# A linear-attention and SiLU kernel: first-layer blocks issued as two halves of 256 columns, finer zero matmuls, and a re-ordered start

## The chip, the cores and the metric

The kernel runs on one core of a Trainium2 chip. A core has a matrix engine (PE, whose weight loads are shown apart as PEld), a vector engine (DVE), a scalar engine (ACT), GpSimd (POOL) and a sync engine (SP), which here issues most of the transfers. Each engine takes its instructions in a fixed order; they meet only through semaphores. The metric is device time in microseconds (us) of one execution.

## The reference, cut to what matters

A decayed linear attention over 4 batches, 8 heads, 768 steps and 48 channels gives rows of 384 numbers. They go through a two-layer network with SiLU:

```python
y[:, :, t] = einsum('bhd,bhde->bhe', rt, state + u * kt (x) vt)
state      = w * state + kt (x) vt          # for t = 0 .. 767
x = y.transpose(0, 2, 1, 3).reshape(3072, 384)
h = x @ w_in                                # 384 -> 2048
out = (h * sigmoid(h)) @ w_out              # 2048 -> 384
```

`(x)` is the outer product over two channel axes. The output is 3072 x 384 in float32.

## The kernel before, in words

The 768 steps are cut into 6 chunks of 128. A *unit* is one chunk of one batch: unit i is chunk i // 4, batch i % 4, so there are 24. Each unit's r, k and v are loaded (`ld`, L71) into one of 8 buffers of each kind, r and k are turned by TensorE (`turn`, L352, transposes at L272), multiplied by powers of the decay on DVE (L289), multiplied with each other on TensorE (L380 for the first units, L455 later), masked, multiplied with v (L396, L552, L561), and added to a bonus term (`vu`) when they leave PSUM (L401). The bonus and the decayed k come from POOL (L240, L245, L248, L258), with a sum over channels on DVE in between (`bonus_sum`, L253).

The attention rows of a chunk are turned into x, 128 channels by 512 steps. For the first four units this is done on TensorE (`yT`, L591) and a copy out of PSUM (`copy_x`, L593); later by a transposing transfer (L584). The first layer then runs per block `ft` of 128 of the 2048 columns: three matmuls over the 384 channels into one PSUM bank (`l1_mm`, L601, L606), and one SiLU on ACT (L615). A block covers all four batches of the chunk, 512 columns (`first`, L679, for chunks 2 to 5), or two blocks at a time with two batches each, 256 columns per matmul (`halved`, L686, and `rest_first`, L676, for chunk 1; part of chunk 0). The second layer (L628) adds 16 matmuls of 384 columns per batch.

For the first six units the order of every instruction is written out by hand in the string `order` (L717). `T`, `P`, `V`, `yT` are TensorE steps, `rT`, `kT`, `n`, `e`, `rd` DVE steps, `ku`, `ru`, `kc`, `vu` POOL steps, `lr`, `lk`, `lv` loads of r, k, v on SP's queue, `v16` the cast of v to float16 on ACT, `pa` and `pd` the zeroing of a buffer's unused columns on ACT or on DVE, `tab` the load of the SiLU table on ACT, `L` and `G` a first-layer block's matmuls and its SiLU, `H` one entry of `halved`. `spin` (L178) issues matmuls of zeros, whose result is not used; the words `6*spin`, `1*spin`, `2*spin` place 15 of them, each of 512 columns.

From unit 6 on a loop takes two units at a time. It interleaves the attention's steps with first- and second-layer pieces from a queue, `fillers`, from which `fill(n)` (L668) pops n pieces in order: before the output matmuls (L782), after the loads (L801) and at two later places. SP's queue holds the loads in the order in which the program issues them, and each of them waits until the transfer issued eight places earlier has landed.

Of the kernel before, what the change touches and what calls it, by code (L numbers as in the profile page):

```python
# [8 lines left out]
FP = mybir.dt.float32  # L9
# [7 lines left out]
def kernel(  # L17
# [11 lines left out]
    nc = tc.nc  # L29

    B, H, S, D = r.shape
    C = 128
# [6 lines left out]
    NFT = DFF // 128  # L39
    NQ = HD // 128  # L40
# [7 lines left out]
    ps = ctx.enter_context(tc.tile_pool(name="ps", bufs=1, space=bass.MemoryType.PSUM))  # L48
    ctx.enter_context(tc.manual_schedule())

    def unit(i):
        return divmod(i, B)
# [15 lines left out]
    win = [big.tile([128, NQ, 512], F16, name=f"win{g}") for g in range(4)]  # L68
# [36 lines left out]
    idle = cst.tile([128, 512], F16)  # L105
# [53 lines left out]
    lamC = cst.tile([128, H, D], FP)  # L159
    lamH = cst.tile([128, H, D], FP)  # L160
# [4 lines left out]
    lamN = cst.tile([128, H, D], FP)  # L165
# [9 lines left out]
            nc.scalar.copy(out=dst[i][:, :, D:64],  # L175
                           in_=idle[:, 0:128].rearrange("p (h d) -> p h d", h=H))

    def spin(n):  # L178
        zs = ps.tile([128, 512], FP, name="zs", tag="moe", bufs=4)
        for _ in range(n):  # L180
            nc.tensor.matmul(zs, idle[:, 0:128], idle, start=True, stop=True)

    def clear():
        for t in att:
# [18 lines left out]
    def spread_row(name, src):  # L203
        spread[name] = ps.tile([128, HD], FP, name="bc", tag="moe", bufs=4)
        nc.tensor.matmul(spread[name], ones, src, start=True, stop=True)
# [91 lines left out]
    def by_planes(i):  # L297
        return i > 2 * B + 1
# [11 lines left out]
    def cast_k(i, copy=nc.scalar.copy):  # L310
        copy(out=kc[i % NIN][:, :, 0:D], in_=kd[i % 2].rearrange("p (h d) -> p h d", h=H))
# [155 lines left out]
    def sums(i):  # L467
        sc, b = unit(i)
        xs = range(2 if sc < NCH - 1 else 1)
        L(i)["sp"] = [ps.tile([128, 512], FP, name="sp", tag="moe", bufs=4) for _ in xs]  # L470
        for p in range(NP):
            for e in range(2):
                for x in xs:
                    rows = slice(HC * x, HC * x + HC)
                    for j in range(2):
                        h = 2 * p + j
                        c0 = (e * NP + p) * D
                        nc.tensor.matmul(L(i)["sp"][x][64 * j:64 * j + 64, c0:c0 + D],  # L478
                                         kc[(i + e) % NIN][rows, h, :],
                                         L(i + e)["v16"][rows, h, :],  # L480
                                         start=True, stop=True)
# [93 lines left out]
    xts = {}  # L575
# [23 lines left out]
    hpss = {}  # L599

    def l1_mm(sc, b0, nb, ft):  # L601
        m = B // nb
        hps = hpss[b0, ft] = ps.tile([128, m, nb * C], FP, name="hps", tag="moe", bufs=4)
        for f in range(m):
            for q in range(NQ):
                nc.tensor.matmul(hps[:, f, :].rearrange("p (b t) -> p b t", b=nb), win[(ft + f) // 4].rearrange("p q (t c) -> p q t c", c=4)  # L606
                                 [:, q, :, (ft + f) % 4],
                                 xts[sc][:, b0:b0 + nb, q, :],
                                 start=(q == 0), stop=(q == NQ - 1))

    def l1_silu(sc, b0, nb, ft):
        if sc not in gts:
            gts[sc] = wrk.tile([128, NFT, B * C], F16, name="gT", bufs=2)
        m = B // nb
        nc.scalar.activation(out=gts[sc][:, ft:ft + m, b0 * C:(b0 + nb) * C], in_=hpss[b0, ft],  # L615
                             func=AF.Silu)

    def l1(sc, b0, nb, ft):
        l1_mm(sc, b0, nb, ft)
        l1_silu(sc, b0, nb, ft)  # L620
# [47 lines left out]
    def fill(n):  # L668
        for _ in range(n):
            if fillers:  # L670
                fillers.pop(0)()
# [5 lines left out]
        return [lambda ft=ft: l1(sc, 2, 2, ft) for ft in range(0, NFT, 2)]  # L677

    def first(sc):  # L679
        return [lambda f=f: l1(sc, 0, B, f) for f in range(NFT)]  # L680

# [2 lines left out]
    halved = [lambda ft=ft: l1(1, 0, 2, ft) for ft in range(0, NFT, 2)]  # L686

    def piece(word, f):
        b0, ft = word.split(".")
        f(0, *blocks[b0], int(ft))  # L690
# [6 lines left out]
        "wy": lambda: columns(nc.scalar, wpT, w, 0), "lnw": powers_r, "eK": exponents_k,  # L697
        "lamK": powers_k, "uc": copy_u, "wb": lambda: spread_row("w", w_row),
        "ub": lambda: spread_row("u", u_row), "lnwb": ln_w, "lamC": powers_c, "lamH": powers_h, "lamN": powers_n,
        "tab": silu_table, "clear": clear, "spin": lambda: None, "H": lambda: halved.pop(0)(),  # L700
    }
    unit_steps = {
        "T": turn, "rT": lambda i: decay_one(i, 0), "kT": lambda i: decay_one(i, 1),
# [12 lines left out]
    }  # L716
    order = """  # L717
        ur kz0 id itr lr0 wy pd0 ak0 cz2 kz3 itc wr mk wx cz1 mh lnw eK cg3 lamK kz4 kz1 lk1
        id16 lr1 pd3 lr3 lk3 clear 6*spin lv0 cg0 lv1 kz7 lr2 ak2 ku0 lv3 lr5 kz2 lv2 ub pd1 lv4
        lr4 lk4 lv5 pd2 lk5 lk7 lr6 lk6 uc T0 1*spin T1 lr7 lv7 kT0 pa4 rT0 ru0 ku1  # L720
        v160 pd5 lv6 rT1 kz6 rd0 kT1 wb ru1 P0 n0 2*spin rd1 P1 vu0 lnwb T2 n1 v161 2*spin
        pd7 lamC lamH lamN pa6 i_q0 V0 v162 tab rT2 e0 kT2 ku2 T3 1*spin yT0 V1 kz5 vu1 i_q1 ru2
        xTD0 e1 P2 yT1 kT3 rd2 rT3 ku3 xTD1 P3 ru3 n2 rd3 v163 n3 L0.0 vu2 kc0 1*spin G0.0
        vu3 V2 L0.2 V3 G0.2 L0.4 e2 i_q2 e3 kc1 yT2 yT3 S0 G0.4 xT2 xTD3 kc2 L0.6 L2.4 G0.6
        st0 L2.0 scA0 v164 kc3 L2.6 ku4 i_q3 v165 L2.2 T4 rT4 kT4 G2.4 ru4 G2.2 T5 G2.0 G2.6
        L4.8 G4.8 L4.10 kT5 G4.10 L4.9 kc4 ku5 S2 L4.11 rd4 rT5 st2 sc2 kc5 sd4 ru5 G4.9
        G4.11 rA4 vu4 i_o0 Q4 D4 rA5 s1_4 ku7 L4.12 rd5 vu5 m4 s2_4 G4.12 L4.13 G4.13 T6 Z4
        L4.14 G4.14 L4.15 z4 yT4 2*spin yT5 i_o2 i_o1 ku6 xT4 xT5 rT6 T7 G4.15 rT7 v167 sd6
        kT6 v166 ru6 lr8 kc6 kc7 H H rd6 i_o3 H vu6 lr9 rP7 rA6 sn4 H H lk8 lk9 sx4 lv9 lv8
        ru7 kT7  # L730
    """
    for word in order.split():
        if "*" in word:
            n, word = word.split("*")
            spin(int(n))
        if word in steps:
            steps[word]()
        elif word[0] == "L":
            piece(word[1:], l1_mm)
        elif word[0] == "G":  # L740
            piece(word[1:], l1_silu)
        else:
            unit_steps[word[:-1]](int(word[-1]))
# [4 lines left out]
    for i in range(B + 2, NU, 2):  # L748
        sc, b = unit(i)
        nxt = range(i + 2, min(i + 4, NU))  # L750
        after = range(i + 4, min(i + 6, NU))
        split = i + 2 < NU and by_planes(i + 2)
        sums(i)
        product_halves(i)
        state_first(i)
        masked_halves(i)
        state_second(i)
        if by_planes(i + 4) and not by_planes(i):
            rescale_state(i)
        if i == B + 2:  # L760
            bonus_sum(i + 1)
            bonus_v(i + 1)
        if i == 2 * B:
            for n in nxt:
                split_k(n, nc.scalar.copy)
        if split:
            turn_planes()
        if b and split:
            for n in nxt:
                cast_k(n)  # L770
                cast_v(n)
        for n in nxt:
            bonus_products(n)
            if not split:
                decayed_k(n)
        if i > B + 2 or sc < NCH - 1:
            next_state(i)
        if not b and split:
            for n in nxt:
                cast_k(n, nc.gpsimd.tensor_copy)  # L780
                cast_v(n, nc.gpsimd.tensor_copy)
        fill(3 if b and split else 4)  # L782
        outputs_halves(i)
        next_crossed(i)
        for n in nxt:
            turn(n)
        evict_halves(i)
        turn_y_dma(i)
        if b:
            fillers.extend((first(sc) if sc > 1 else rest_first(sc)) + second(sc))  # L790
        for n in nxt:
            if split:
                decay_one(n, 0)
                if b:
                    join_k(n)
            else:
                decay(n)
        for dst, src in ((kin, k), (rin, r), (vin, v)):
            for n in after:
                ld(n, dst, src)  # L800
        fill(4)  # L801
        if i > 2 * B and not b and split:
            for n in nxt:
                join_k(n)
        for n in nxt:
            bonus_sum(n)
            if not split:
                cast_v(n)
            bonus_v(n)
        for n in after:  # L810
            weighted_k(n)
        if after and by_planes(i + 4) and not i == B + 2:
            for n in after:
                split_k(n)
        for n in nxt:
            fill(2)
            decay_r16(n, True)
        if i == 2 * B and split:
            for n in nxt:
                join_k(n)  # L820
        fill((5 if b and split else 4) if i < NU - 4 else 2)
# [31 lines left out]
```

## Time and profile before

| | us |
|---|---|
| median of 3 runs | 185.99 (183.11, 185.99, 186.72) |
| the profiled execution: its own time | 185.49 |
| its span, first to last instruction | 183.8 |
| PE busy in the span | 174.5 |
| POOL busy | 129.3 |
| DVE busy | 117.0 |
| ACT busy | 115.8 |

The profiled execution's own time is 1.69 us more than its span, which lies around it. Matmuls are pipelined: the duration of one holds the time until its result is out, so the cost of one in a row of many is the time from start to start. In the chain of waits each line has the start, the time that the piece adds to the chain, and what it is. In the timeline each line has start, length, engine, line and operation, and in brackets the time that the engine sat idle before it, with what ended the wait. A queue (SPq, POOLq) stands for the issuing of transfers.

### The profile page before, as it was taken

Reading aid. Unit: us, or ns where it says so; the run is one execution under the profiler, and the core shown is the slowest. Engines: PE = TensorE matmul, PEld = TensorE weight load, DVE = VectorE, ACT = ScalarE, POOL = GpSimd, SP = SyncE. Lnnn points to the kernel's source line nnn. Section 1 sums busy time; section 2 is a strip of 40 time slices with the busy share of each in tenths; the row PEclk is TensorE's granted clock in tenths of the full one; section 3 lists DMA queues with packets and bytes.
Section 4 is the critical chain, followed back from the end, with each engine's and each line's share of the span. In section 5 each row is a group of like instructions: output and inputs, shape, how many; then the busy total and the mean of one; then the engine's idle time right before and its main releaser. Section 6 shows DMA issues by size and latency. Waiting matters only on the chain.

```text
span 183.8 us, 6611 instructions
## 1 busy us (share of the span) xinstructions
PE 174.5 (95%) x2801; PEld 113.9 (62%) x2801; DVE 117.0 (64%) x231; ACT 115.8 (63%) x208; POOL 129.3 (70%) x179
## 2 busy tenths in 40 slices
PE   7977899999899999999899999999999999999993
PEld 2555786588666976656556555657656566555562
DVE  5999728897977985865775955776944974000120
ACT  4471787699145797398597488797588781299200
POOL 7999999898899979869979769879769700000000
PEclk9999999999999999999999999999999999999999
DMA  5999999899697799999599999499799201410022
GB/s 95 238 192 216 178 175 200 154 224 225 129 189 210 114 202 184 199 183 202 114 178 177 162 209 213 92 183 160 183 197 250 49 4 46 128 43 0 10 79 86
DMA packets 102865, 27.89 MB, mean 152 GB/s; under 512 B 97586, under 2 KB 102324, under 8 KB 102836
## 3 DMA queue, kind: packets, MB, share of 16 engines
q1 hardware_dynamic: 98224, 23.86, 66.5%
q0 software_dynamic: 2176, 3.15, 10.1%
q10 hardware_dynamic: 2436, 0.46, 1.3%
q8 instruction: 22, 0.36, 0.8%
q14 instruction: 7, 0.06, 0.1%
HBM read 20.45 MB, written 4.72 MB: 137 GB/s over the span
## 4 chain that ended last, share of the span: by engine, by line
PE 72%; POOL 17%; DMA 5%; issue 5%; ACT 0%; POOLq 0%
PE ops L628 33%; PE hps L606 26%; DMA kin<-in_k_dram 5%; PE att L455 4%; POOL ku L240 4%; POOL rku_f L245 3%; PE att L272 3%; POOL vu L258 2%; POOL kc L248 2%; PE yp L552 2%; PE sp L478 2%; PE ops L653 1%; PE yp L561 1%; POOL win L84 1%; POOL wout L89 1%
## 5 line engine op out<-in xcount | busy, mean ns | idle before, releaser
L606 PE MATMUL hps<-xT,win 128*128 128x512 f16 (+1 forms) x360 | 66.3, 338 | 0.1
L615 ACT ACTIVATE gT<-hps 128x512 f16<-128x512 f32 x96 | 55.3, 597 | 12.2 <-PE hps L606 8.9
L628 PE MATMUL ops<-wout,gT 128*128 128x384 f16 x368 | 62.9, 326 | 0.1
L606 PEld LDWEIGHTS <-win 128*128 128x128 f16 x360 | 39.0, 114 | 21.1 <-issue 0.4
L628 PEld LDWEIGHTS <-gT 128*128 128x128 f16 x368 | 35.0, 98 | 23.9 <-ACT gT L615 0.8
L401 DVE TENSOR_TENSOR y<-yp,vu 64x384 f16<-64x384 f32 (+1 forms) x34 | 18.9, 555 | 11.3 <-PE yp L561 5.5
L245 POOL TENSOR_TENSOR rku_f<-ku,u_bc 128x384 f32<-128x384 f32 x24 | 24.2, 1010 | 1.4
L240 POOL TENSOR_TENSOR ku<-kin,rin 128x384 f32<-128x384 f32 x24 | 24.2, 1007 | 0.7 <-DMA rin<-in_r_dram 0.6
L258 POOL TENSOR_TENSOR vu<-vin,rku 128x384 f32<-128x384 f32 x24 | 19.6, 828 | 6.8 <-DVE rku L253 6.8
L289 DVE TENSOR_TENSOR rT<-att,lamR 112x512 f16<-112x512 f32 (+1 forms) x26 | 17.8, 684 | 4.2 <-PE att L272 3.8
L326 ACT COPY kT<-blocks 112x1024 uint16<-112x1024 uint16 x14 | 15.6, 1160 | 7.6 <-DMA blocks<-planes 7.5
L634 ACT COPY osb<-ops 128x384 f32<-128x384 f32 x20 | 9.4, 475 | 16.5 <-PE ops L628 12.5
L495 DVE TENSOR_TENSOR s<-sp,sdec 112x384 f32<-112x384 f32 x10 | 5.6, 557 | 16.0 <-PE sp L478 15.4
L636 DVE COPY osb<-ops 128x384 f32<-128x384 f32 x3 | 1.7, 557 | 21.3 <-PE ops L628 21.3
L462 DVE TENSOR_TENSOR am<-att,maskH 128x1024 f16<-128x1024 f32 x10 | 12.2, 1224 | 3.5 <-PE att L455 3.5
L343 DVE TENSOR_TENSOR rX<-att,lamR 48x256 f16<-48x256 f32 x32 | 13.5, 421 | 0.5
L263 ACT CAST v<-vin 128x384 f16<-128x384 f32 x16 | 7.9, 510 | 8.4 <-DMA vin<-in_v_dram 8.3
L253 DVE TENSOR_REDUCE rku<-rku_f 128x8 f32<-128x384 f32 x24 | 12.4, 542 | 0.9 <-POOL rku_f L245 0.9
L314 POOL TENSOR_TENSOR lnw_bc<-kin,lamN 128x384 f32<-128x384 f32 x7 | 7.0, 1001 | 8.0 <-DMA kin<-in_k_dram 6.4
L434 ACT CAST s1h<-s 48x384 f16<-48x384 f32 x16 | 8.2, 510 | 6.7 <-DVE s L495 6.6
L455 PE MATMUL att<-rT,kT 48*64 48x64 f32 x640 | 11.9, 220 | 0.2 <-issue 0.2
L455 PEld LDWEIGHTS att<-rT,kT 48*64 48x64 f32 x640 | 10.6, 135 | 0.3 <-issue 0.3
(106 smaller groups left out, 214.0 us busy)
## 6 DMA issues: line engine op xcount, KB each, us to landing
rin<-in_r_dram SPq DMA_DIRECT2D x24, 192.0 KB, 4.0
vin<-in_v_dram SPq DMA_DIRECT2D x24, 192.0 KB, 4.6
out_dram<-osb SPq DMA_DIRECT2D x23, 192.0 KB, 3.2
kin<-in_k_dram SPq DMA_DIRECT2D x22, 192.0 KB, 3.5
win<-in_moe_w_in_dram POOLq DMA_DIRECT2D x4, 384.0 KB, 6.3
wout<-in_moe_w_out_dram POOLq DMA_DIRECT2D x4, 384.0 KB, 6.6
kin<-in_k_dram ACTq DMA_DIRECT2D x2, 192.0 KB, 3.7
xT<-y SPq DMA_TRANSPOSE x9, 2.8
```

Source lines behind the costliest of these rows:

```text
L240: eng.tensor_tensor(out=L(i)["ku"], in0=kin[i % NIN][:, :, 0:D], in1=rin[i % NIN][:, :, 0:D], op=ALU.mult)
L245: eng.tensor_tensor(out=L(i)["rku_f"], in0=L(i)["ku"], in1=u_bc, op=ALU.mult)
L253: nc.vector.tensor_reduce(out=L(i)["rku"], in_=L(i)["rku_f"], axis=mybir.AxisListType.X, op=ALU.add)
L258: eng.tensor_tensor(out=L(i)["vu"], in0=vin[i % NIN], in1=L(i)["rku"].unsqueeze(2).broadcast_to([128, H, D]), op=ALU.mult)
L289: nc.vector.tensor_tensor(out=L(i)[key].rearrange("p g (y t) -> p y g t", y=2), in0=L(i)["t"][0:PR, :, x], in1=lam, op=ALU.mult)
L326: nc.scalar.copy(out=L(i)["kT"].rearrange("p g t -> p (g t)").bitcast(U16) .rearrange("p (n y) -> p n y", y=2), in_=turned[0:PR, i % 2].re ...
L343: nc.vector.tensor_tensor(out=rx[here], in0=L(i)["t"][there, x, 0], in1=(lamM if by_planes(i) else lamR)[there, :, 0:HC], op=ALU.mult)
L401: nc.vector.tensor_tensor(out=y16[a], in0=y[b, 0:HD], in1=vu[a], op=ALU.add)
L455: nc.tensor.matmul(a[o0:o0 + HC, j, e, p, :], kT[r0:r0 + D, p, HC * x:HC * x + HC], rT[r0:r0 + D, p, HC * x:HC * x + HC], start=True, stop ...
L606: nc.tensor.matmul(hps[:, f, :].rearrange("p (b t) -> p b t", b=nb), win[(ft + f) // 4].rearrange("p q (t c) -> p q t c", c=4) [:, q, :, ( ...
L615: nc.scalar.activation(out=gts[sc][:, ft:ft + m, b0 * C:(b0 + nb) * C], in_=hpss[b0, ft], func=AF.Silu)
L628: nc.tensor.matmul(opss[b], gts[sc][:, ft, b * C:(b + 1) * C], wout[:, ft, :], start=(ft == 0), stop=(ft == NFT - 1))
```

## The change

1. A new function `l1_halves` replaces `l1` for the blocks of chunks 2 to 5 (16 blocks each): a block's three matmuls of 512 columns become six of 256, first for batches 0 and 1, then for batches 2 and 3, into the two halves of the same PSUM bank. The SiLU stays one instruction per block.
2. `spin` issues zero matmuls of 100 columns, five for each one before; the first six keep 512 columns (`long`). So nine of 512 become 45 of 100.
3. The start's order: `lv2` goes ahead of `lr5`; the zeroing of unit 7's columns goes from DVE to ACT (`pd7` to `pa7`); `v162` moves from before the table load to behind the two x copies; the x copies of units 0 and 1 go from DVE to ACT (`xTD` to `xT`); `rT3` goes ahead of `rd2`.
4. In the loop at unit 6, `fill` pops five pieces before the output matmuls instead of four, and three after the loads instead of four.

```diff
-    def spin(n):
+    def spin(n, cols=100):
         zs = ps.tile([128, 512], FP, name="zs", tag="moe", bufs=4)
-        for _ in range(n):
-            nc.tensor.matmul(zs, idle[:, 0:128], idle, start=True, stop=True)
+        for _ in range(n * (512 // cols)):
+            nc.tensor.matmul(zs[:, 0:cols], idle[:, 0:128], idle[:, 0:cols], start=True, stop=True)
...
+    def l1_halves(sc, ft):
+        hps = hpss[0, ft] = ps.tile([128, 1, B * C], FP, name="hps", tag="moe", bufs=4)
+        for b0 in range(0, B, 2):
+            for q in range(NQ):
+                nc.tensor.matmul(hps[:, 0, b0 * C:(b0 + 2) * C].rearrange("p (b t) -> p b t", b=2),
+                                 win[ft // 4].rearrange("p q (t c) -> p q t c", c=4)[:, q, :, ft % 4],
+                                 xts[sc][:, b0:b0 + 2, q, :],
+                                 start=(q == 0), stop=(q == NQ - 1))
+        l1_silu(sc, 0, B, ft)
...
     def first(sc):
-        return [lambda f=f: l1(sc, 0, B, f) for f in range(NFT)]
+        return [lambda f=f: l1_halves(sc, f) for f in range(NFT)]
...
-        id16 lr1 pd3 lr3 lk3 clear 6*spin lv0 cg0 lv1 kz7 lr2 ak2 ku0 lv3 lr5 kz2 lv2 ub pd1 lv4
+        id16 lr1 pd3 lr3 lk3 clear 6*long lv0 cg0 lv1 kz7 lr2 ak2 ku0 lv3 lv2 kz2 lr5 ub pd1 lv4
...
-        pd7 lamC lamH lamN pa6 i_q0 V0 v162 tab rT2 e0 kT2 ku2 T3 1*spin yT0 V1 kz5 vu1 i_q1 ru2
-        xTD0 e1 P2 yT1 kT3 rd2 rT3 ku3 xTD1 P3 ru3 n2 rd3 v163 n3 L0.0 ...
+        lamC lamH lamN pa6 pa7 i_q0 V0 tab rT2 e0 kT2 ku2 T3 1*spin yT0 V1 kz5 vu1 i_q1 ru2
+        xT0 e1 P2 yT1 kT3 rT3 rd2 ku3 xT1 v162 P3 ru3 n2 rd3 v163 n3 L0.0 ...
...
-            spin(int(n))
+            spin(int(n), *((512,) if word == "long" else ()))
...
-        fill(3 if b and split else 4)
+        fill(5 if i == B + 2 else 3 if b and split else 4)
...
-        fill(4)
+        fill(3 if i == B + 2 else 4)
```

More of the change, by code (lines that the diff above doesn't have):

```diff
@@ L699 @@
         "ub": lambda: spread_row("u", u_row), "lnwb": ln_w, "lamC": powers_c, "lamH": powers_h, "lamN": powers_n,
-        "tab": silu_table, "clear": clear, "spin": lambda: None, "H": lambda: halved.pop(0)(),
+        "tab": silu_table, "clear": clear, "spin": lambda: None, "long": lambda: None, "H": lambda: halved.pop(0)(),
     }
@@ L718 @@
         ur kz0 id itr lr0 wy pd0 ak0 cz2 kz3 itc wr mk wx cz1 mh lnw eK cg3 lamK kz4 kz1 lk1
-        id16 lr1 pd3 lr3 lk3 clear 6*spin lv0 cg0 lv1 kz7 lr2 ak2 ku0 lv3 lr5 kz2 lv2 ub pd1 lv4
-        lr4 lk4 lv5 pd2 lk5 lk7 lr6 lk6 uc T0 1*spin T1 lr7 lv7 kT0 pa4 rT0 ru0 ku1
-        v160 pd5 lv6 rT1 kz6 rd0 kT1 wb ru1 P0 n0 2*spin rd1 P1 vu0 lnwb T2 n1 v161 2*spin
-        pd7 lamC lamH lamN pa6 i_q0 V0 v162 tab rT2 e0 kT2 ku2 T3 1*spin yT0 V1 kz5 vu1 i_q1 ru2
[L723 to L730, printed above, removed]
+        id16 lr1 pd3 lr3 lk3 clear 6*long lv0 cg0 lv1 kz7 lr2 ak2 ku0 lv3 lv2 kz2 lr5 ub pd1 lv4
+        lr4 lk4 lv5 pd2 lk5 lk7 lr6 lk6 uc T0 1*spin T1 lr7 lv7 kT0 pa4 rT0 ru0 ku1 v160 pd5 lv6
+        rT1 kz6 rd0 kT1 wb ru1 P0 n0 2*spin rd1 P1 vu0 lnwb T2 n1 v161 2*spin lamC lamH lamN pa6
+        pa7 i_q0 V0 tab rT2 e0 kT2 ku2 T3 1*spin yT0 V1 kz5 vu1 i_q1 ru2 xT0 e1 P2 yT1 kT3 rT3
+        rd2 ku3 xT1 v162 P3 ru3 n2 rd3 v163 n3 L0.0 vu2 kc0 1*spin G0.0 vu3 V2 L0.2 V3 G0.2 L0.4
+        e2 i_q2 e3 kc1 yT2 yT3 S0 G0.4 xT2 xTD3 kc2 L0.6 L2.4 G0.6 st0 L2.0 scA0 v164 kc3 L2.6
+        ku4 i_q3 v165 L2.2 T4 rT4 kT4 G2.4 ru4 G2.2 T5 G2.0 G2.6 L4.8 G4.8 L4.10 kT5 G4.10 L4.9
+        kc4 ku5 S2 L4.11 rd4 rT5 st2 sc2 kc5 sd4 ru5 G4.9 G4.11 rA4 vu4 i_o0 Q4 D4 rA5 s1_4 ku7
+        L4.12 rd5 vu5 m4 s2_4 G4.12 L4.13 G4.13 T6 Z4 L4.14 G4.14 L4.15 z4 yT4 2*spin yT5 i_o2
+        i_o1 ku6 xT4 xT5 rT6 T7 G4.15 rT7 v167 sd6 kT6 v166 ru6 lr8 kc6 kc7 H H rd6 i_o3 H vu6
+        lr9 rP7 rA6 sn4 H H lk8 lk9 sx4 lv9 lv8 ru7 kT7
     """
```

## The prediction

> **What bounds the kernel now.** I read the page first, then the chain of waits, then the busy time in five stretches, and last the timelines of the start.
>
> ```profile
> span 183.8 us, 6611 instructions
> ...
> PE 174.5 (95%) x2801; PEld 113.9 (62%) x2801; DVE 117.0 (64%) x231; ACT 115.8 (63%) x208; POOL 129.3 (70%) x179
> ...
> PEclk9999999999999999999999999999999999999999
> ```
>
> PE is busy for 95% of the span at a granted clock of 9 tenths or more in every slice, so the idle 9.3 us are all that a better order could win. The stretches (length, busy time of each engine, granted clock, DMA) say where they lie:
>
> ```profile
> 0.00:5.60 5.60, 4.31 (x12) 1.62 (x12) 3.33 (x15) 2.94 (x7) 4.51 (x24) 1.00 0.67 124
> 5.60:22.30 16.70, 13.82 (x268) 10.21 (x267) 15.42 (x29) 8.26 (x19) 16.55 (x23) 1.00 1.12 208
> 22.30:48.20 25.90, 24.73 (x522) 19.35 (x522) 18.76 (x37) 19.68 (x39) 23.91 (x29) 1.00 1.05 192
> 48.20:180.80 132.60, 131.60 (x2004) 82.75 (x2004) 79.53 (x152) 84.68 (x144) 84.32 (x106) 1.00 0.71 140
> ```
>
> From 48.2 to 180.8 PE works 131.6 of 132.6 us: there each ns added to a matmul is added to the end. From 5.6 to 22.3 it idles 2.9 us, and POOL works 16.55 of 16.70: that stretch is POOL's. From 22.3 to 48.2 PE idles 1.2 us. The last 3.0 us are a copy and a store, which the change does not touch. The chain of waits has the pieces that price the change:
>
> ```profile
> 38.46 9.68 DMA kin<-in_k_dram
> 48.14 0.04 issue
> 48.19 0.44 PE att L272 x8
> 48.62 7.91 PE ops L628 x48
> ...
> 59.94 0.66 PE hps L606 x6
> ...
> 61.83 4.71 PE hps L606 x42
> ...
> 101.51 0.43 issue
> ...
> 159.99 10.36 PE hps L606 x48
> ```
>
> The reader is to see that the chain runs through POOL and one load of k until 48.14 and through PE alone behind it, and that L606 stands in it with both sizes: x42 and x6 are matmuls of 256 columns (chunk 1), x48 is of 512.
>
> **Part by part.**
>
> *Halves.* Chunks 2 to 5 have 4 x 16 blocks of 3 matmuls, 192 of 512 columns; they become 384 of 256. From the chain, 512 columns cost 10.36 / 48 = 215.8 ns from start to start, and 256 columns 4.71 / 42 = 112.1 ns. The form is the same as that of the new function: two batches, a new weight for each matmul, half a PSUM bank. A pair costs 224.2 ns, 8.4 more, and 192 x 8.4 ns = +1.61 us, nearly all behind 48.2 where PE has no slack. Bounds: the short run, 0.66 / 6 = 110.0 ns, gives +0.8 us; the run of 30 in the start (timeline below, from 22.63 to the next start at 26.03) gives 113.3 ns and +2.1 us. I take 112.1, the longest run in the stage itself. The gain that the halves could bring, a start on batches 0 and 1 before batches 2 and 3 are there, has no wait to remove: the list of groups by form has 0.0 us idle before L606 of 512 columns.
>
> ```profile
> L606 PE MATMUL hps<-xT,win 128*128 128x512 f16 x216 | 49.2, 380 | 0.0
> L606 PE MATMUL hps<-xT,win 128*128 128x256 f16 x144 | 17.1, 273 | 0.1
> ```
>
> ```profile
> L606 PEld LDWEIGHTS <-win x360: 111/113/134, 18.2 to 169.8; 128*128 128x128 f16 x180
> ```
>
> Of each group the number behind the first bar is the busy time and the mean, behind the second the idle time before it. The weight load has a duration (least, median, most) of 111, 113 and 134 ns. Beside a 512-column matmul it is hidden with 100 ns to spare; beside 256 columns nothing is to spare, and the 112.1 ns already hold that. [...]
>
> *The start.* TensorE, DVE, ACT and POOL around the moved steps:
>
> ```profile
> 12.04 0.44 PE L272 MATMUL att<-ident,rin 64*112 64x64 f32 x8 [1.11 <-DMA rin<-in_r_dram]
> ...
> 14.19 0.33 PE L591 MATMUL yT<-ident,y 128*128 128x128 f16 x3
> 14.36 0.36 PE L396 MATMUL yp<-v,am 128*128 128x48 f16 x8
> ...
> 17.14 1.09 PE L380 MATMUL att<-rT,kT 48*64 48x128 f32 x32 [1.02 <-DVE rT L289]
> ...
> 22.30 0.40 PE L419 MATMUL sp<-v,kc 128*64 128x48 f16 x14 [0.35 <-POOL kc L248]
> 22.63 3.47 PE L606 MATMUL hps<-xT,win 128*128 128x256 f16 x30
> 26.03 0.44 PE L272 MATMUL att<-ident,rin 64*112 64x64 f32 x8
> ...
> 37.12 0.59 PE L181 MATMUL zs<-idle 128*128 128x512 f16 x2
> 37.55 0.34 PE L591 MATMUL yT<-ident,y 128*128 128x128 f16 x3
> ...
> 48.19 0.44 PE L272 MATMUL att<-ident,kin 64*112 64x64 f32 x8 [0.56 <-DMA kin<-in_k_dram]
> ```
>
> ```profile
> 14.62 0.34 DVE L595 COPY xT<-yT 128x384 f16<-128x384 f16 x1
> 14.88 0.55 DVE L401 TENSOR_TENSOR y<-yp,vu 128x384 f16<-128x384 f32 x1
> ...
> 15.95 0.54 DVE L253 TENSOR_REDUCE rku<-rku_f 128x8 f32<-128x384 f32 x1
> 16.41 0.68 DVE L289 TENSOR_TENSOR rT<-att,lamR 112x512 f32<-112x512 f32 x1
> ```
>
> ```profile
> 13.23 0.29 ACT L175 CAST kin<-idle 128x128 f32<-128x128 f16 x1
> 17.77 0.51 ACT L263 CAST v<-vin 128x384 f16<-128x384 f32 x1 [4.24 <-DMA vin<-in_v_dram]
> 18.30 1.28 ACT L227 ACT_TABLE_LOAD   x1
> ...
> 22.00 0.47 ACT L595 COPY xT<-yT 128x384 f16<-128x384 f16 x1
> ```
>
> ```profile
> 17.88 0.83 POOL L258 TENSOR_TENSOR vu<-vin,rku 128x384 f32<-128x384 f32 x1
> ...
> 21.23 2.92 POOL L248 TENSOR_TENSOR kc<-kin,lamC 128x384 f16<-128x384 f32 x3
> ```
>
> Ahead of `rT3` the x copy goes (14.62 to 14.88, 0.26 us) and the reduction steps behind it (15.95 to 16.41, 0.46 us), so product 3 starts 0.72 us sooner, near 16.4. ACT waits 4.24 us for unit 2's v and only then loads its table; with `tab` ahead of `v162`, the table load (1.28 us) and two x copies (0.47 us each on ACT) fall into that wait, and `lv2` one place earlier on SP lets v land earlier. `pa7` is two copies of 0.29 us in the same wait. The reduction, now after `rT3`, ends near 16.9, before POOL wants it at 17.88; `lr5` one place later loads what unit 5's turn wants only behind unit 4's at 26.03. All of it reaches the end only past PE's next wait, and that is for the decayed k of unit 1 (22.30), the first of three POOL operations that start at 21.23, in a row that POOL works through without idling. POOL's order is unchanged. So I take 0 of the 0.72 us: the wait at 22.30 grows from 0.35 to about 1.1 us. Bounds: 0 to -0.72 us.
>
> *Zero matmuls.* 100 columns lie, by columns of the 512 price, at 42 ns (215.8 x 100 / 512); from above, the 128-column turns of y, three from 14.19 to 14.36, at 57 ns. Five cost 0.21 to 0.29 us against 0.215 for one before (37.12 to 37.55 for two). Seven of the nine spins stand before 22.30, where the waits at 12.04, 17.14 and 22.30 take the difference in; the two at 37.12 add 0 to 0.14 us, and I take +0.10, near the turns, which also load a weight each. If all nine counted it would be +0.6 us. [...]
>
> *Five pieces at unit 6.* At 48.19 the turn of unit 9's k waits 0.56 us for its load, which landed at 48.14. A fifth piece ahead of it is four L628 matmuls, 4 x 7.91 / 48 us = 0.66 us, so PE arrives at about 48.3, after the landing: -0.56 us, and the piece is gone from behind. If the load lands later, as much of the gain goes. What moves back with it, unit 6's outputs and the turning of its y, is used by the first layer at 61.83, far off.
>
> *Sum.* 185.49 (span 183.8 and 1.69 around it) + 1.61 - 0 + 0.10 - 0.56 = 186.64, I say 186.6 us. The profiled execution stands 0.50 us under the median of the three runs; a run as slow as the median would give 187.1.
>
> **The rivals.**
>
> *The start's gain is kept.* If POOL gets ahead too, the 0.72 us reach the end, and with the cheaper halves (+0.8) the sum is 185.49 + 0.8 - 0.72 + 0.1 - 0.56 = 185.1; with the dearer, 185.9. For it: DVE and ACT do get ahead. Against it: POOL idles 0.15 us in that whole stretch. A gain over 2% is not in reach: all of PE's idle time between 5.6 and 48.2 is 4.05 us, and the halves take 1.6 of it back.
>
> *The weight loads become the bound (slower).* With half the columns over which to hide, the load's 113 ns are no longer covered where loads slow down. If each matmul took the longest load, 134 ns, a pair would cost 268, 52 more: 192 x 52 ns = +10.0 us, 195.0 in all. It decides from 3.7 us on, 2%, so from (3.7 + 0.5) / 192 = 22 ns a pair, 118.7 ns a matmul. With every added load open, 192 x 113 ns = +21.7 us and 206.7 would result. [...] Against both: 42 matmuls at 112.1 in the same stage. Chance 8 in 100.
>
> *Instruction supply, the same sign.* The change adds 228 matmuls with as many weight loads to 2801. PE already stops twice for nothing but its instructions:
>
> ```profile
> 88.05 0.34 PE L561 MATMUL yp<-v,am 64*64 64x48 f16 x19 [0.51 <-issue]
> ```
>
> The other such stop, at 101.51 in the chain, took 0.43 us. Two more of these would give 187.6. Chance 12 in 100.
>
> *The halves change nothing and unit 6's wait stays (the change does not do what it says).* If the load of k lands later by what PE gains, the sum without -0.56 is 187.2; it is part of my own case.
>
> **How the numbers follow.** My forecast with its bounds (185.7, cheap halves and spins at nothing, to 187.7, dear ones and the wait kept) has 62 in 100, the kept start 18, the supply stops 12, the open loads 8. The three runs of the kernel before spread by -1.6% and +0.4% about their median, and I take the same for the kernel after: the lower end is 185.1 less 0.7 = 184.4, the upper end 187.6, by 0.7 of spread and 0.6 of a third stop, 188.9. About 2% is what a measurement of this kernel can tell from no change. Faster by over 2% comes only from the kept start and a lucky spread: 5 in 100. Slower by over 2% is the open loads with 8, and 6 for the spread on top of the supply stops: 14. Within 2%: 81.
>
> **What the profile after would show.** L606 from 160 on in runs of 96 with 112 ns from start to start: right; 120 or more, and the weight loads are the bound. PE's wait for `rT3` at 17 us gone, and its wait for the decayed k at 22.3 grown to about 1.1: right; start of that matmul before 22: the start's gain is kept. No wait for k ahead of unit 9's turn near 48. A granted clock below 9 tenths anywhere, or idle time behind 48.2 above 2 us, would make the prediction wrong.

## The result and the profile after

Over 22 runs each, the changed kernel has a median of 186.96 us and the kernel before 185.02 us. The ratio is 1.0118, with a 95% interval of 1.0092 to 1.0143: about 2.2 us slower, within the 2% that were called no change. Of the profile after first the page (the halves' matmul is L615 there, and lines behind it are 10 up):

```profile
span 183.8 us, 7064 instructions
...
PE 175.1 (95%) x3029; PEld 135.3 (74%) x3029; DVE 116.1 (63%) x227; ACT 117.6 (64%) x212; POOL 129.4 (70%) x179
...
q8 instruction: 23, 0.38, 0.9%
...
L615 PE MATMUL hps<-xT,win 128*128 128x256 f16 x384 | 44.2, 273 | 0.7 <-DMA xT<-y 0.7
```

The span is 183.8 us, as long as that of the kernel before. The two spans say nothing on the ratio: this execution is the fastest of the 22 of the changed kernel (185.51 us), while the one shown of the kernel before (185.49 us) is slower than the median of its own 22. What the traces are good for is to see what each wait is made of. TensorE's waits after (total, times, longest) and its stretch behind 48.2 us:

```profile
PE att L272 <- DMA rin<-in_r_dram: 1.6, 1, 1.6
...
PE sp L419 <- POOL kc L248: 0.7, 1, 0.7
PE hps L615 <- DMA xT<-y: 0.7, 2, 0.5
PE att L455 <- issue: 0.6, 1, 0.6
PE att L380 <- DVE rT L289: 0.5, 1, 0.5
```

```profile
48.20:180.80 132.60, 131.85 (x2208) 102.81 (x2202) 80.42 (x154) 85.09 (x144) 84.77 (x106) 1.00 0.76 140
```

The wait for `rT3` halved (1.02 to 0.5 us) and that for the decayed k doubled (0.35 to 0.7). That is the way that was forecast, though the first was to be gone and the second to reach 1.1. The wait for k ahead of unit 9's turn is gone. New is a wait that the kernel before did not have: the first layer (L615) waits for the transposed x. The DMA share behind 48.2 us rose from 0.71 to 0.76 with the same 140 GB/s: the same bytes took longer. In the chain of waits the x transfers now stand ahead of the first layer:

```profile
64.19 4.53 DMA kin<-in_k_dram
...
70.83 1.53 POOL planes L317 x2
...
76.15 4.02 DMA xT<-y
80.22 3.11 PE hps L615 x27
...
102.73 4.53 DMA xT<-y
107.30 3.11 PE hps L615 x27
...
115.75 4.71 PE hps L615 x42
...
129.78 4.39 DMA xT<-y
...
159.89 10.48 PE hps L615 x96
```

A transposing transfer of x takes 4.0 to 4.5 us here. In the view of the transfers, asked for one flight of x each (kind of queue with packets, MB and share; then issues with the time to landing), the x of unit 8 in the kernel before, then in the changed kernel:

```profile
q1 hardware_dynamic: 1880, 0.62, 91.7%
...
xT<-y SPq DMA_TRANSPOSE x1, 2.8
```

```profile
q1 hardware_dynamic: 2026, 0.63, 111.4%
q8 instruction: 1, 0.02, 2.2%
...
xT<-y SPq DMA_TRANSPOSE x1, 4.5
```

The reader is to see the row of q8. It is a packet of 16 KB of instructions. There are 22 of them in the kernel before, which has 2 x 2801 matmuls and weight loads, 255 for each packet, and 23 in the changed kernel with 2 x 3029, 263 for each: by this count, and by the stops further down, it is TensorE's program that comes in over the same 16 DMA engines (0.8% and 0.9% of their time). In the changed kernel such a packet starts in the flight of x of units 8, 10, 14, 16 and 18; in the kernel before only in that of units 10, 14 and 18. With a packet in its flight the x of unit 8 took 4.5 us against 2.8 without, and TensorE too stands still behind some packets, 0.20 to 1.65 us, as its stops further down show.

### The profile page after: what moved, and what is told of

It is laid out like the page before. It is cut to its first block, busy times and chain, and to the rows that moved or that the text cites. A ratio compares the mean times of both kernels' runs of the same rounds, so it can differ in the third digit from the quotient of the medians.

```text
span 183.8 us, 7064 instructions
## 1 busy us (share of the span) xinstructions
PE 175.1 (95%) x3029; PEld 135.3 (74%) x3029; DVE 116.1 (63%) x227; ACT 117.6 (64%) x212; POOL 129.4 (70%) x179
## 4 chain that ended last, share of the span: by engine, by line
PE 42%; POOL 35%; DMA 12%; issue 7%; DVE 3%; SPq 0%; POOLq 0%; ACT 0%
PE hps L615 22%; PE ops L638 13%; POOL ku L240 7%; DMA xT<-y 7%; POOL rku_f L245 6%; DMA kin<-in_k_dram 5%; POOL kc L248 4%; POOL vu L258 4%; PE att L455 3%; DVE y L401 2%; POOL sdec L516 2%; POOL win L84 2%; POOL planes L317 2%; POOL u_wide L314 2%; PE ops L663 1%
## 5 line engine op out<-in xcount | busy, mean ns | idle before, releaser
L615 PE MATMUL hps<-xT,win 128*128 128x256 f16 x384 | 44.2, 273 | 0.7 <-DMA xT<-y 0.7
L615 PEld LDWEIGHTS <-win 128*128 128x128 f16 x384 | 41.5, 113 | 2.1 <-issue 1.2
L606 PE MATMUL hps<-xT,win 128*128 128x256 f16 (+1 forms) x168 | 23.1, 289 | 0.0
L606 PEld LDWEIGHTS <-win 128*128 128x128 f16 x168 | 17.6, 114 | 2.4 <-issue 0.2
```

The lines of the kernel that those rows point to most:

```text
L615: nc.tensor.matmul(hps[:, 0, b0 * C:(b0 + 2) * C].rearrange("p (b t) -> p b t", b=2), win[ft // 4].rearrange("p q (t c) -> p q t c", c=4)[ ...
```

## The experiments

All ratios are against the kernel before, run in the same rounds on the same chip, with 95% intervals. The three groups below (each part alone; all four and all but one; the place of the packets) ran on three chips. A run stands for 12 executions, but for 6 with all four parts and with all but the fill counts.

**Each part alone.** The halves:

```diff
-        return [lambda f=f: l1(sc, 0, B, f) for f in range(NFT)]
+        return [lambda f=f: l1_halves(sc, f) for f in range(NFT)]
```

> Only the halves of chunks 2 to 5 are taken over; start, zero matmuls and fill as before. By the prediction's sum this is the dear part: +1.6 us (bounds +0.8 to +2.1), ratio 1.0045 to 1.011, with 109 to 113 ns from start to start for 256 columns. Rival A, that the halves cost all of the 2.2 us and more through waits for the transposed x in the first layer: ratio 1.012 or more, and idle time before the halves' matmuls that ends on the transfer of x. Rival B, that the new order of the start is the loss: here only 192 x 2.6 ns = 0.5 us, ratio 1.003 or less.

Measured: 0.9996 (0.9965 to 1.0027). The halves alone cost nothing that can be told, below the prediction's +1.6 us and far below rival A. The chain of this run:

```profile
88.12 4.71 PE hps L615 x42
...
158.84 10.48 PE hps L615 x96
```

At the end 96 halves take 10.48 us, 109.2 ns each, 218.3 a pair against 215.8 for one of 512 columns: 2.5 ns, and 192 of them 0.5 us.

The zero matmuls (nine of 512 columns become 45 of 100):

```diff
-            spin(int(n))
+            spin(int(n), *((512,) if word == "long" else ()))
```

> Only the zero matmuls change: nine of 512 columns become 45 of 100. By the prediction: +0.1 us (0 to 0.6), not to be told from 1.000 within 0.3%. Rival: the clock's state in the start hangs on these, and the ratio moves by more than 0.5% with a lower mean clock.

Measured: 1.0027 (0.9988 to 1.0067), not clear of 1.000. The granted clock of its profile is 1.00 in every stretch, as in the kernel before, so the rival's lower clock is not there. The profile has a wait for x ahead of the first layer, which neither theory had:

```profile
81.02 3.43 PE L606 MATMUL hps<-xT,win 128*128 128x512 f16 x15 [1.22 <-DMA xT<-y]
```

The start's order:

```diff
...
-        xTD0 e1 P2 yT1 kT3 rd2 rT3 ku3 xTD1 P3 ru3 n2 rd3 v163 n3 L0.0 ...
+        xT0 e1 P2 yT1 kT3 rT3 rd2 ku3 xT1 v162 P3 ru3 n2 rd3 v163 n3 L0.0 ...
...
```

> Only the start's order changes (v of unit 2 early, table early, x copies and unit 7's zeroing on ScalarE, rT3 ahead of rd2). By the prediction: 0, at best -0.7 us, ratio 0.996 to 1.000, because PE waits for POOL's decayed k at 22.3 us anyway. Rival B: the load of v ahead of that of r lets r of unit 2 land later (its wait was 1.56 us in the changed kernel against 1.11), POOL and PE follow, and the ratio is 1.004 or more.

Measured: 0.9983 (0.9953 to 1.0013). Rival B, that the order is the loss, falls.

The fill counts:

```diff
-        fill(3 if b and split else 4)
+        fill(5 if i == B + 2 else 3 if b and split else 4)
...
-        fill(4)
+        fill(3 if i == B + 2 else 4)
```

> Only the five and three pieces at unit 6. By the prediction: -0.56 us, ratio 0.997, because the wait for k ahead of unit 9's turn is covered. Rival C: most executions do not have that wait, and the ratio is 1.000.

Measured: 0.9972 (0.9947 to 0.9997), which looks like the forecast gain; no later run shows it again (below).

The product of the four is 0.998. The changed kernel is at 1.0118. The loss is in parts acting together.

**All four, and all but one.**

> The changed kernel once more, all four parts together. If the parts add, the product of the four ratios measured alone (0.9996, 1.0027, 0.9983, 0.9972) gives 0.998, half a us faster than before. If it measures 1.009 or more again, as in the first comparison, the loss of some 2 us lies in parts acting together, and one of the next three, which leave one part out each, falls back to 1.000.

Measured: 1.0113 (1.0072 to 1.0154). The loss is there again.

Without the halves (`first` calls `l1` as before):

> All but the halves: zero matmuls, start's order and fill changed, first layer in 512 columns. Theory X (the loss needs the halves, which put a first matmul on x of batches 0 and 1 and a later wait on x of batches 2 and 3 inside a block): ratio 1.000. Theory Y (the loss is made in the start or by the fill): ratio 1.009 or more still.

Measured: 1.0059 (1.0024 to 1.0094), between X and Y: by the middle values the halves are part of it, not all. The interval overlaps that of all four, so how large a part is not told.

Without the fine zero matmuls (512 columns as before):

> All but the zero matmuls of 100 columns: halves, order and fill changed. If the zero matmuls take part in the loss (alone they measured 1.0027, the worst of the four): ratio near 1.000. If not: 1.009 or more.

Measured: 1.0038 (1.0005 to 1.0072). Most of the loss goes with the zero matmuls, which alone cost 0.5 us at the most likely value.

Without the new fill counts (four and four at unit 6):

> All but the fill counts: halves, zero matmuls and order changed, four and four pieces at unit 6. By the prediction the fill gains 0.56 us, so without it the ratio is 0.003 above that of all four together. Theory Z (the fill moves unit 6's outputs back and with them the transposed x and the loads, which all later units inherit): ratio near 1.000.

Measured: 1.0112 (1.0074 to 1.0151), the same as all four, and theory Z falls. A worth of 0.56 us, 0.3%, is less than either interval can tell.

In the ten profiles up to here every kernel with the fine zero matmuls (five) waits for x in the first layer, 0.5 to 1.7 us, and none without them does. The zero matmuls stand ahead of 38 us, the waits behind 78 us. What could reach so far is the place of the instruction packets: 36 more matmuls with 36 weight loads move all later packets by 72 instructions. The halves matter in another way. A pair of units has 176 attention matmuls (32 + 64 + 32 + 32 + 16 in the chain) and, on average, 32 of the second layer and 24 of the first: 232, with weight loads 464 instructions. With the halves it is 48 in place of 24, 256 matmuls and 512 instructions, two packets to a pair. So before, the packets' place drifts from pair to pair and hits the flight of x only here and there; with the halves the place that the start has set stays, hit or miss, through all chunks. That was the theory (Q) for the last four. In the packet lists of the first two profiles the packet nearest to the issue of x starts from 2.39 us ahead of it to 2.32 behind it in the kernel before (units 8 to 22), and in the changed kernel 0.98 to 2.53 us behind it for units 8 to 20 and 1.15 ahead for unit 22.

**The place of the instruction packets.** Four short zero matmuls behind each of the nine later ones, and nothing else (`few` is 4, and 0 for the first six):

```diff
-        for _ in range(n):
-            nc.tensor.matmul(zs, idle[:, 0:128], idle, start=True, stop=True)
+        for m in range(n * (1 + few)):
+            cols = 16 if m % (1 + few) else 512
+            nc.tensor.matmul(zs[:, 0:cols], idle[:, 0:128], idle[:, 0:cols], start=True, stop=True)
```

> The kernel before, with its nine zero matmuls of 512 columns kept, and four more of only 16 columns behind each: as many instructions as the change adds there (36 matmuls and 36 weight loads, 72), almost no columns. Theory Q: what counts is the number of TensorE instructions. They come in by transfers of 16 KB, 256 instructions each, and 72 more at the start move these transfers into the flight of the transposed x of units 8 and 10. Then both of these land 4.0 us or more after their issue (2.75 without), PE waits about 1.2 us for x near 80 us, and the ratio is that of the zero matmuls alone or above, 1.003 to 1.008. Rival: the columns or the clock count; then x lands after 2.75 to 3.3 us, there is no such wait, and the ratio is 1.000 to 1.002.

Measured: 1.0057 (1.0018 to 1.0095). The x of units 8 and 10 take 4.3 and 4.1 us, each with an instruction packet in its flight, and TensorE waits 0.9 us for the second (its line numbers are one up):

```profile
PE hps L607 <- DMA xT<-y: 0.9, 1, 0.9
```

The granted clock of this execution is 0.90 on average from 5.6 to 22.3 us, but that of the halves alone and of the fill alone is 0.90 there too, without a wait for x, and the fine zero matmuls alone have the wait at 1.00. So added instructions bring the late x and the wait, with hardly a column added. The ratio alone would not tell: the short zero matmuls take time too. Where they stand open, two long and eight short ones take 0.64 us from the first to the next row (0.43 for two long ones), 26 ns for a short one, and 36 of them would make 0.9 us if all counted.

All four parts, with the later zero matmuls in 256 columns:

```diff
-    def spin(n, cols=100):
+    def spin(n, cols=256):
```

> The changed kernel with all four parts, but the later zero matmuls in 256 columns, two for each one before: 18 instructions more than before instead of 72. Theory Q: with the halves a pair of units has exactly 512 TensorE instructions, two such transfers, so the phase that the start sets stays; 18 leaves it close to that of the kernel without the fine zero matmuls, all transposed x land in 2.75 to 3.6 us, nothing waits for x, and the ratio falls from 1.0113 to about 1.003, the halves' own cost of some 0.6 us. Rival, that zero matmuls of part of the columns as such or the moved order are the loss: 1.008 or more.

Measured: 0.9957 (0.9922 to 0.9991). That one number, which takes 27 zero matmuls away, turns 1.1% of loss into 0.4% of gain against the kernel before. It is the lowest ratio of the study, though the intervals of the order alone and of the fill alone hold it too. Its columns are those of the changed kernel to within 2% (18 x 256 against 45 x 100), and where they stand open they take the same 0.44 us: the number of instructions is what differs. Its waits, the transfers in the flight of x of unit 10, and the first layer behind it:

```profile
PE hps L606 <- DMA win<-in_moe_w_in_dram: 1.6, 2, 1.2
PE att L186 <- DVE idle L108: 1.3, 1, 1.3
PE att L272 <- DMA rin<-in_r_dram: 1.1, 1, 1.1
PE att L380 <- DVE rT L289: 0.5, 1, 0.5
```

```profile
q1 hardware_dynamic: 2367, 0.74, 103.5%
...
xT<-y SPq DMA_TRANSPOSE x1, 2.8
```

```profile
77.79 3.44 PE L615 MATMUL hps<-xT,win 128*128 128x256 f16 x30
```

No q8, 2.8 us, no wait for x, and 30 halves in a row. All its x transfers land after 2.7 to 2.8 us.

Eight short zero matmuls in place of four:

> As the kernel with four short zero matmuls behind each, but with eight: 144 instructions more than before. Theory Q: twice the shift moves the transfers of instructions on, ahead of the flight of x of units 8 and 10, so the wait for x near 80 us is gone and the kernel with more work is the faster of the two, ratio 0.999 to 1.003. Rival, that each added instruction or zero matmul costs: slower than the one with four, 1.006 or more.

Measured: 1.0084 (1.0044 to 1.0124). Half of the expectation held: there is no wait for x in its profile (x of unit 10 lands after 2.97 us). The total missed: the rival's 1.006 or more came, and the theory had priced the additions in the start at nothing. In the profile r of unit 2 lands 5.5 us after its issue (4.5 in the kernel before), the last 18 zero matmuls take 0.83 us in place of 0.43, and unit 6's sums start at 43.31 us against 41.82. Part of that delay may belong to this execution alone: its granted clock is 0.90 on average from 5.6 to 22.3 us, against 1.00 in the kernel before. So late x is not needed for a loss of this size, and how much of the 1.0084 is the plain time of 72 more short matmuls is not shown.

The two parts that add no TensorE instruction, order and fill:

> Only the start's order and the fill counts are changed: the two parts that add no TensorE instruction. If the parts add: 0.9983 x 0.9972 = 0.9955, 0.8 us faster than before. If the instruction transfers alone made the differences: between 0.995 and 1.000, with no wait for x near 80 us.

Measured: 1.0003 (0.9969 to 1.0036), no wait for x. The 0.9955 of the sum did not come; the two small gains measured alone were not real, or not additive. The interval still holds a gain of 0.3%, so the forecast -0.56 us is not excluded; beside the fill alone, no run shows it.

**What the fourteen traces say together.** Taken from the lists of packets: 80 flights of x with both ends in the trace, by the start of the nearest instruction packet relative to the issue of x.

```text
packet starts                       flights   x lands after (us)
0.4 to 2.2 us behind the issue          23      3.50 to 4.54
0.9 us ahead to 0.4 behind it           25      2.73 to 3.63
earlier, later or none                  32      2.73 to 2.84
```

In the three profiles with the halves and 45 fine zero matmuls together the DMA share behind 48.2 us is 0.76, in the other eleven 0.69 to 0.73.

The load of r of unit 2, issued near 7.5 us, goes the same way: with the first instruction packet at 9.7 to 10.6 us (six kernels, the changed one among them) it lands after 4.8 to 5.5 us, with that packet at 11.0 us or later (six) after 3.9 to 4.5. In the profile of the changed kernel unit 2 was turned at 12.87 us, not at 12.04.

The same packets also stop TensorE itself. Its stops called "issue", in which it waits for nothing that the profile names, are 15 in the fourteen traces, 0.20 to 1.65 us long, such as these of the kernel with order and fill and of the changed one:

```profile
33.29 0.33 PE L455 MATMUL att<-rT,kT 48*64 48x64 f32 x3 [1.65 <-issue]
```

```profile
43.23 0.35 PE L455 MATMUL att<-rT,kT 48*64 48x64 f32 x9 [0.59 <-issue]
```

Count TensorE's matmuls and weight loads in order of their start. The first instruction behind a stop is number 949 (five kernels without added zero matmuls, near 33 us), 1461 (five with 72 added instructions, near 43 us), 1717, 2995, 3505, 4017 or 4527: every time 175 to 181 past a multiple of 256. Every time it starts 1.2 to 1.6 us behind the end of an instruction packet, and it is the packet of the same count: the 3rd for number 949, which is 181 past 3 x 256, the 5th for 1461, the 17th for 4527. So at these places TensorE waited for its own program. The fastest version, with 256 columns, has no such stop and no wait for x in its profile.

## Why the prediction was right, and where it was not

The time and the sign were right: 186.6 us forecast, 186.96 measured, within 2%. The way there was not, and that the time came so near is luck. The forecast adds 1.15 us to an execution of 185.49 us, which lies 0.47 us above the median of that kernel's 22 runs; the change measured is 2.2 us. Of the terms, the halves were too dear by 1.1 us, the gain of 0.56 us was not found, and what the added instructions do was put at nothing.

- *Halves, +1.61 us: mis-sized.* They cost 0.5 us by the chain. The failed step is "From the chain, 512 columns cost 10.36 / 48 = 215.8 ns from start to start, and 256 columns 4.71 / 42 = 112.1 ns": the two rows come from different places. Where the 42 stand, right behind a unit's transposes, 512 columns cost more too. The kernel before, at such a place:

```profile
88.98 4.66 PE hps L606 x21
```

221.9 ns each, against 224.3 for a pair of halves there (4.71 x 2 / 42): 2.4 ns, as at the end (2.5).
- *"has no wait to remove"*: true, and not the whole question. In the changed kernel an instruction packet starts 0.98 to 2.53 us behind the issue of x of each of the units 8 to 20, and x is late in all five of these flights whose landing the trace shows (4.0 to 4.5 us): the late x came again in every round that can be read, up to unit 18.
- *Zero matmuls, +0.10 us: the step that failed most.* It priced columns, and these cost nothing: ten of 100 columns took as long as two of 512 (in the changed kernel's timeline below 0.44 us from the first row's start to the second's; 0.43 before).

```profile
36.64 0.60 PE L181 MATMUL zs<-idle 128*128 128x100 f16 x10
37.08 0.34 PE L591 MATMUL yT<-ident,y 128*128 128x128 f16 x3
```

What the step left out is where the added instructions put the packets, and that acts far from the start: zero matmuls ahead of 38 us, waits for x behind 78 us. With the halves, order and fill the ratio is 1.0113 with the 72 added instructions, 1.0038 with none and 0.9957 with 18: it does not go by the number. That the place decides is shown for the late x, not for all of the time: the 0.8% between none and 18 are not explained; neither profile has a wait for x or a stop, and the waits for the first layer's weights (2.4 and 1.6 us) are two executions.
- *The start, 0 of 0.72 us: right in the sum.* The wait moved from `rT3` to the decayed k, and order alone is 0.9983 with 1.000 inside the interval. Not by the steps alone, though: r of unit 2 landed late, and the matmul on the decayed k started at 22.96 us, 0.66 later than before. That was made up, as two waits of the kernel before (0.40 us near 27, 0.20 near 32) did not come: unit 6's sums start at 41.35 us against 41.82, and the stop of 0.59 us follows. And the new order has a wait of TensorE that the prediction did not name, for the weights of the first layer (`win`, near 18 to 22 us): 0.3 to 2.4 us in six of the eight profiles with it, none in the six others.
- *Five pieces, -0.56 us: not found.* With and without them the changed kernel is at 1.0113 and 1.0112. The wait for k ahead of unit 9's turn belonged to that one execution; none of the other thirteen profiles has it.
- *Weight loads as the bound: refuted.* 109.2 ns a half leaves no open load of 113. The loads run beside the matmuls: in the profile after they are busy for 135.3 us and the matmuls for 175.1, in a span of 183.8.
- *Instruction supply*, a rival with 12 in 100, had the right matter and only half of what it does. TensorE does run dry at a packet, but the change did not add two such stops: the profile before has three, 1.14 us in sum, the one after has one of 0.59. What came on top is that transfers beside a packet are late (x after 3.50 to 4.54 us against 2.73 to 2.84). That two stops at +0.9 us are not far from what x cost in the profiles (0.5 to 1.7 us) is chance.

Shown is that 72 instructions in the start, with hardly a column, bring the late x and the wait; that fewer zero matmuls in the changed kernel take both away, and its loss; and that no flight clear of an instruction packet (the last row of the table) is longer than 2.84 us. Not shown is how a packet of 16 KB, 0.9 to 2 us long, holds a transfer up by 1.7 us; which of the engines it uses was not tried. Of the 2.6 us between the spans of the changed kernel and of its version with 256 columns, the two profiles place 0.55 us in the start (unit 6's sums at 41.35 against 40.80 us), 0.8 in the stop for instructions right behind and 0.7 in waits for x; the rest is not placed. These are single executions, and that of the changed kernel is its fastest.

## What to carry to other kernels

Count instructions, not only columns, when cheap work is cut finer: here a packet of 16 KB came in over the data's DMA engines for every 255 to 263 matmuls and weight loads, x landed after 3.50 to 4.54 us with such a packet 0.4 to 2.2 us behind its issue, against 2.84 at the most clear of one, and TensorE itself stopped for 0.20 to 1.65 us behind some of them. A stop with no cause in the profile is worth a count: here each stood 175 to 181 instructions past a multiple of 256. If, as with the halves here, a round of the loop has nearly a whole number of packets (512 instructions, two packets), look at whether one starts in the same flight in every round: with all four parts and 72 instructions added in the start x was late in all five flights from unit 8 to unit 18 whose landing the trace shows, with 18 added no x took longer than 2.8 us. So try two or three counts. And compare rows of the same place in the pipeline when a difference of 2% of a matmul decides.

## What the runs showed of the hardware that was not expected

- In the 80 flights of the table a transposing transfer of 6 x 128 x 128 float16 landed after 2.73 to 2.84 us clear of an instruction packet, after 2.73 to 3.63 us with one from 0.9 us ahead of its issue to 0.4 behind it, and after 3.50 to 4.54 us with one 0.4 to 2.2 us behind it.
- A matmul of 256 columns with a new weight took 109.2 ns from start to start, 96 in a row (10.48 us, the halves alone and the changed kernel); one of 100 columns with its weight load 44 ns (ten in 0.44 us, the changed kernel), one of 16 columns 26 ns (eight in 0.21 us, the kernel with four short ones behind each).
- In the fourteen traces TensorE's 15 stops with no named cause, 0.20 to 1.65 us long, stand 175 to 181 matmuls and weight loads past a multiple of 256, and end 1.2 to 1.6 us behind the end of the instruction packet of the same count.
- One execution's waits are not the kernel's: of PE's waits in the first profile, that for k near 48 us is in none of the thirteen others.
